# An attention and two-MLP kernel: planner latencies and keys exchanged, the low half of the probabilities written in one step

## The chip, the core and the metric

The kernel runs on one core of a Trainium2 chip. The metric is device time in microseconds. Engines are named PE (matmul), DVE (vector), ACT (scalar), POOL (GpSimd) and SP, whose queue issues all DMAs.

## The reference

Inputs `q`, `k`, `v` have shape (4, 8, 576, 64): 4 batches, 8 heads, 576 tokens. The weights are 512 x 2048 and 2048 x 512, twice, in float64.

```python
q_rot, k_rot = rotate(q), rotate(k)                 # rotary embedding
scores = (1 / sqrt(64)) * q_rot @ k_rot.T
attn = softmax(scores)                              # max subtracted, 1e-9 in the sum
x = (attn @ v) -> 2304 x 512
h = x @ w_in;  x = (h * sigmoid(1.702 * h)) @ w_out     # first MLP
h = x @ w_in2; y = where(h > 0, h, exp(min(h, 0)) - 1) @ w_out2   # second MLP
```

## The kernel before

**Numbers.** Every matmul operand is split into a high and a low float16 half; a product is the sum of three (high x high, high x low, low x high), so that float32 precision is nearly kept. Low halves are made on DVE as `value * scale - high`.

**Attention.** Work is cut into 144 *units*: a block of tokens `n` (two per batch, 320 or 256 tokens), a pair of heads `hp`, a chunk of 128 queries and one head of the pair (or the last 64 queries of both heads). A unit (`s_unit`) runs: scores on PE (L788) into one of 2 PSUM buffers, negative maximum on DVE (L792), bias on DVE (L796), exponential on ACT (L800) into one of 2 buffers E, two tiny steps on DVE (L807, L811), the normalised high half on ACT or DVE (L816, L820), the low half on DVE, and a DMA transpose from SP (L836, L839) into `et`. The tile `Ehl` holds 576 high columns and 576 low ones. The low part is stored turned: its last 64 keys come first (L830, 64 columns), then its first 512 (L829). After the transpose the nine 128-row slots of `et` are thus: high keys 0 to 511 in four slots, one slot with the 64 last high keys in its upper and the 64 last low keys in its lower half, and low keys 0 to 511 in four slots.

For each block and head pair, `av_unit` multiplies the nine slots by V in 28 matmuls (L982): high slots by both halves of V, low slots by V's high half. The tile `v16` holds V's two halves; its fifth slot has the last 64 keys twice, once per half of the partitions. V's high half is made on ACT (L764), its low half on DVE (L768), 16 times each (batch, head pair).

**Preparation.** `prep` runs 16 times: loads of q and k (L607, L608) into one buffer R, maximum (L614) and scale, rotation on DVE (L631, L635, L639), high halves on ACT (L653, L659), low halves on DVE (L664), and one transpose of 3840 columns into `qkT` (L681).

**MLPs.** Weights arrive as float64 bit patterns and are converted on ACT and DVE (L421 to L440), their maximum is taken, then they are split (L497 to L524). The raw weights of the first MLP pass through the tiles `gh` and `gl`, which the first MLP itself writes later: it can start only when the conversion of `w1o` is over. The first MLP runs block by block (L1028, then L1062), with L1031, L1035, L1039 and L1045 on ACT and DVE between. When attention is done its memory is given to the second MLP's weights (`open2`), which are then loaded, converted and split; the second MLP runs in blocks of 512 tokens (L1169, L1210).

**Order.** Each engine runs its instructions in program order, and that order is written by a planner (`Plan.run`): a list scheduler that gives each operation a price per engine and a key, and on an engine that is free starts the ready operation with the lowest key. An operation is ready when all its predecessors are over, which the planner puts a latency `lat` (345 ns; `lsame`, 218 ns, on the same engine) after their end. A DMA has its own latency plus `dlat`, 823 ns. The keys come from the table `TUNE`: for unit `i`, scores have `i - TUNE["s"]`, maxima `i - TUNE["mx"]`, high and low halves `i`. The first MLP's matmuls have 1e6 and more on PE, so they fill what attention leaves; their work on ACT and DVE has -1e5 to -9e4 and goes first.

Of the kernel before, what the change touches and what calls it, by code (L numbers as in the profile page):

```python
# [9 lines left out]
F16 = mybir.dt.float16  # L10
# [4 lines left out]
ALU = mybir.AluOpType  # L15
AX = mybir.AxisListType
P = 128
# [9 lines left out]
    pe_w1i=12, pe_w1o=0, lsame=218.42826132665004, tab=-30.0, f_dve=8.919624976581842, f_act=-17.90165985370676, f_pool=12.224437399728332,  # L27
    w2s=15.07761611796668, w1i2=30.204632970574707, w1o2=-73.74635818936522, dlat=823.3988909607715, qh=-8.32414955715731,
    kt=-6.667322173378593, vam=7.40425146733344, p0=2, lat=344.9241913205742, slack=1000000000.0, w1i=-56.15596474631266,
    w1i_s=2.8429601770045223, w1o=19.54548776828132, w1o_s=0.9651873495458939, prep0_s=1.3779993771618317, nt=5.6622832505119804,  # L30
    s_f=40.3256386921686, mx_f=6.7540349396707375, ex_f=7.075547533776429, av_f=14.806376760777082, prep0=29.665311617753602,
    prep=-52.798465949313695, va0=1.3429180038713335, va=-3.8436751296349594, vs=0.9879982807500122, tiny=0.9993537914172514,
    av=-30.965081688981684, ex=-2.7284093806181335, mx=2.7048753351162738, s=-9.997660299005439, tr=-10.34413763597054,
    bits=-9.409726003447773,
)
ORDER = ("pe", "act", "dve", "pool", "dma", "none")
# [6 lines left out]
class Plan:  # L43
# [12 lines left out]
    def op(self, eng, *args, port=False, **kw):  # L56


        lat = TUNE["lat"]
# [29 lines left out]
    def run(self):  # L89
# [10 lines left out]
        def start(e, now):  # L100
# [39 lines left out]
            busy[e] = end  # L140
            if e == "pool" or (e == "dve" and o.port):
                busy["port"] = end
            heapq.heappush(events, (end, o.seq, 0, e, None))
            if e != "dma":
                heapq.heappush(events, (end + min(TUNE["lsame"], o.lat), o.seq, 0.5, e, o))
            heapq.heappush(events, (end + o.lat, o.seq, 1, e, o))
# [76 lines left out]
def kernel(  # L223
# [63 lines left out]
    def buf(name, pool, shape, dt, n):  # L287
        plan.buffers(name, n)
        spec[name] = (pool, shape, dt)
# [27 lines left out]
    buf("v16", ap_, [P, 2, 5, 2, D], F16, BUFS["v16"])  # L317
    buf("x", per, [P, 2, NMAX], F16, BUFS["x"])
# [21 lines left out]
    def across(am, n, hM, after, key, add=False, use=()):  # L340
# [23 lines left out]
        o = op({"dve": 220.0 + 150.0 * (n > 1)}, most, [o], key, use=[hM], port=n > 1)  # L364
# [229 lines left out]
    def prep(b, hp):  # L594
# [109 lines left out]
        t = op(*dma_tr(3840), tr, [ql, kl], key - TUNE["kt"], need=[("qkT", hX)], use=[hN])  # L704
# [21 lines left out]
    def v_prep(b):  # L726
# [32 lines left out]
        for hp in range(NP):  # L759
            ks = last_u[fb[b], hp] - TUNE["vs"]  # L760
            h, hv = ("vs", b, hp), ("v16", b, hp)
# [551 lines left out]
```

## Time and profile before

| | us |
|---|---|
| median of 3 runs (1124.43 to 1135.83) | 1132.98 |
| the profiled execution | 1129.07 |
| its span, first to last instruction | 1127.3 |
| busy: PE / DVE / ACT / POOL | 976.1 / 826.4 / 638.4 / 12.3 |
| mean granted clock of PE, as a share of full speed | 0.954 |

A busy share over the whole span is a mean of stages with different limits, so the profile is read by stretches of time. A duration of an operation in the trace can overlap with that of the next on the same engine. A line number is that of the kernel before.

### The profile page before, as it was taken

To read this page: it belongs to the slowest core of one execution; us is meant where nothing else is said; L and a number is where in the kernel's file an instruction comes from. 1 tells how busy PE (TensorE), PEld (TensorE's weight loads), DVE (VectorE), ACT (ScalarE), POOL (GpSimd) and SP (SyncE) were. 2 spreads that over 40 slices of the span, in tenths; PEclk is the share of its full clock that TensorE was granted. 3 is DMA by queue.
4 is the path that set the end of the run, shared out by engine and by line. 5 is a ranking of instruction groups with operands and counts; after the bars stand their busy time and mean duration, and the time that the engine had idled before them with its cause. 6 is when DMAs were issued, how large, how long until landed. Compare 5 with 4: busy or idle time off the path is not lost.

```text
span 1127.3 us, 18484 instructions
## 1 busy us (share of the span) xinstructions
PE 976.1 (87%) x6710; PEld 615.7 (55%) x6710; DVE 826.4 (73%) x2070; ACT 638.4 (57%) x1237; POOL 12.3 (1%) x31
## 2 busy tenths in 40 slices
PE   1356669889858999989899999985999999999998
PEld 0123348656536667867588777732444444444474
DVE  7898899789978979989998679999227227237041
ACT  6588778566667757687475546785225125125041
POOL 2000000000000000000000000000000000000000
PEclk9988769999969989999999999998999999999999
DMA  9989743866756676664665553651000100000000
GB/s 303 227 202 246 148 92 72 161 129 130 171 136 108 148 154 137 126 147 102 139 125 115 144 167 101 191 164 38 19 19 1 47 19 1 28 19 1 19 20 19
DMA packets 287419, 122.19 MB, mean 108 GB/s; under 512 B 261728, under 2 KB 274656, under 8 KB 287328
## 3 DMA queue, kind: packets, MB, share of 16 engines
q1 hardware_dynamic: 287328, 121.02, 46.1%
q8 instruction: 52, 0.85, 0.3%
q14 instruction: 39, 0.32, 0.1%
HBM read 53.35 MB, written 9.44 MB: 56 GB/s over the span
## 4 chain that ended last, share of the span: by engine, by line
PE 43%; DVE 33%; DMA 13%; issue 4%; ACT 3%; SPq 3%; DVEq 0%; POOL 0%; POOLq 0%; ACTq 0%
PE m L1210 17%; PE m L1169 14%; PE m L1062 5%; DVE Ehl L829 4%; DMA qkT<-n 4%; DVE st L792 4%; DVE t L1035 3%; DVE gl L1045 3%; DMA R<-in_k_dram 3%; DMA et<-Ehl 3%; PE av L982 2%; PE m L1028 2%; PE s L788 2%; DVE n L664 2%; DMA R<-in_moe_w_in_dram 1%
## 5 line engine op out<-in xcount | busy, mean ns | idle before, releaser
L1062 PE MATMUL m<-gh,wo 128*128 128x256 f16 (+1 forms) x1024 | 203.0, 290 | 0.1
L1028 PE MATMUL m<-x,wi 128*128 128x256 f16 (+1 forms) x1536 | 198.2, 286 | 5.4 <-DVE t L1035 4.0
L1169 PE MATMUL m<-yhl,w2i 128*128 128x512 f16 (+1 forms) x960 | 188.5, 358 | 4.6 <-DVE e L1180 3.7
L1210 PE MATMUL m<-w2o,g 128*128 128x512 f16 x864 | 190.3, 382 | 0.0
L1028 PEld LDWEIGHTS <-wi 128*128 128x128 f16 x1536 | 149.0, 98 | 47.2 <-issue 9.9
L1062 PEld LDWEIGHTS <-wo 128*128 128x128 f16 x1536 | 150.7, 99 | 42.9 <-issue 3.6
L788 PE MATMUL s<-qkT 128*128 128x288 f16 (+1 forms) x640 | 104.4, 311 | 58.0 <-ACT E L800 41.1
L1062 PE MATMUL m<-gl,wo 128*128 128x256 f16 (+1 forms) x512 | 148.5, 290 | 0.0
L1169 PEld LDWEIGHTS <-w2i 128*128 128x128 f16 x960 | 93.8, 98 | 97.6 <-issue 5.7
L800 ACT ACTIVATE E<-s,st,qk_c 128x576 f32<-128x576 f32 x144 | 118.8, 826 | 43.2 <-DVE st L796 13.2
L1210 PEld LDWEIGHTS <-g 128*128 128x128 f16 x864 | 84.7, 99 | 102.8 <-issue 3.5
L1176 DVE TENSOR_SCALAR e<-e 128x512 f32<-128x512 f32 (+1 forms) x80 | 31.7, 397 | 147.1 <-ACT e L1172 147.1
L792 DVE TENSOR_REDUCE st<-s 128x1 f32<-128x576 f32 x144 | 107.2, 746 | 15.0 <-PE s L788 14.6
L829 DVE SCALAR_TENSOR_TENSOR Ehl<-E,st,Ehl 128x512 f16<-128x512 f32 x144 | 107.1, 744 | 10.5 <-ACT Ehl L816 10.1
L788 PEld LDWEIGHTS <-qkT 128*128 128x128 f16 (+1 forms) x640 | 57.4, 106 | 90.2 <-issue 55.5
L1213 ACT ACTIVATE o<-m,eo 128x512 f32<-128x512 f32 x18 | 12.4, 688 | 157.3 <-PE m L1210 157.3
L816 ACT ACTIVATE Ehl<-E,st 128x576 f16<-128x576 f32 x102 | 78.3, 770 | 38.0 <-issue 11.7
L1172 ACT ACTIVATE e<-m,y_c 128x512 f32<-128x512 f32 (+1 forms) x80 | 51.4, 643 | 52.1 <-PE m L1169 46.3
L982 PE MATMUL av<-et,v 128*64 128x320 f16 (+1 forms) x896 | 73.4, 316 | 3.8 <-DMA et<-Ehl 3.7
L1031 ACT ACTIVATE t<-m,hsc 128x256 f32<-128x256 f32 (+1 forms) x128 | 63.4, 496 | 23.3 <-PE m L1028 21.0
L1183 ACT ACTIVATE g<-e,y_c 128x512 f16<-128x512 f32 (+1 forms) x80 | 53.7, 675 | 25.0 <-DVE e L1180 24.5
L982 PEld LDWEIGHTS <-v 128*64 128x64 f16 x896 | 54.8, 121 | 19.4 <-issue 8.1
(164 smaller groups left out, 1136.7 us busy)
## 6 DMA issues: line engine op xcount, KB each, us to landing
R<-in_moe_w_in_dram SPq DMA_DIRECT2D x16, 512.0 KB, 4.7
R<-in_moe_w_out_dram SPq DMA_DIRECT2D x16, 512.0 KB, 4.3
gh<-in_moe_w_in_dram SPq DMA_DIRECT2D x8, 512.0 KB, 4.8
gl<-in_moe_w_in_dram SPq DMA_DIRECT2D x8, 512.0 KB, 5.8
R<-in_q_dram SPq DMA_DIRECT2D x16, 256.0 KB, 2.9
R<-in_k_dram SPq DMA_DIRECT2D x16, 256.0 KB, 3.5
V<-in_v_dram SPq DMA_DIRECT2D x32, 128.0 KB, 2.9
gh<-in_moe_w_out_dram SPq DMA_DIRECT2D x8, 512.0 KB, 4.2
```

The lines of the kernel that those rows point to most:

```text
L788: nc.tensor.matmul(o, X[:, a, t], X[:, 2 + 2 * x + a, cs], start=x == 0, stop=x == 1)
L792: nc.vector.tensor_reduce(out=st["t"][:, 0:1], in_=take(hS)[:, :, 0:NS], axis=AX.XY, op=ALU.max, negate=True)
L800: nc.scalar.activation(out=take(hE).rearrange("p (c f) -> p c f", c=2), in_=take(hS)[:, :, 0:NS], func=AF.Exp, bias=t[:, 1:2], scale=csc[b ...
L816: nc.scalar.activation(out=X16[:, 0:S], in_=take(hE), func=AF.Copy, scale=st["t"][:, 3:4])
L829: nc.vector.scalar_tensor_tensor(out=X16[:, S + TAIL:2 * S], in0=E[:, 0:512], scalar=r, in1=X16[:, 0:512], op0=ALU.mult, op1=ALU.subtract)
L982: nc.tensor.matmul(ps[64 * a:64 * a + 64, 0:N], V[:, w, j, a, :], T[:, a, blk, 0:N], start=i == 0, stop=i == len(slots) - 1)
L1028: nc.tensor.matmul(ps[:, 0:N], W1i.lhs(kk, u, wl), x[:, xl, 0:N], start=kk == 0 and i == 0, stop=kk == KD - 1 and i == 2)
L1031: nc.scalar.activation(out=take(ht)[:, 0:N], in_=take(hM)[:, 0:N], func=AF.Tanh, scale=hsc[b][:, 1:2])
L1062: nc.tensor.matmul(ps[:, 0:N], W1o.lhs(f, d, wl), (gh, gl)[xl][:, f, 0:N], start=f == 0 and i == 0, stop=f == KF - 1 and i == 2)
L1169: nc.tensor.matmul(ps[:, 0:n], W2i.lhs(kk, u, wl), Y[:, xl, kk, 0:n], start=kk == 0 and i == 0, stop=kk == KD - 1 and i == 2)
L1183: nc.scalar.activation(out=g2_tile()[:, u, 0:n], in_=take(he)[:, 0:n], func=AF.Copy, scale=st["c"][:, 1:2])
L1210: nc.tensor.matmul(ps, g[:, f, 512 * gi + P * tt:512 * gi + P * tt + P], W2o.h[:, f, 512 * wl:512 * wl + 512], start=f == 0 and i == 0, st ...
```

## The change

- The low half of the probabilities is written in key order, 576 columns in one DVE operation in place of 512 and 64. The fifth slot of `et` then holds the last 64 high keys and the *first* 64 low keys, and the four slots after it hold low keys 64 to 575.
- So V is needed shifted by 64 keys for the low slots. A new tile `vsh` (3 buffers) gets V's high half moved across the partitions by two DMAs from SBUF to SBUF, and a third DMA puts V's first 64 keys into the lower half of `v16`'s fifth slot. These three DMAs are issued on SP's queue after L768, 16 times; the attention output waits for them. The number of its matmuls stays 28.
- The planner's latency becomes one per engine (PE 230 ns, ACT 170, DVE 145, POOL 200), at most 125 on the same engine. The transpose into `qkT` is priced 4700 + 1800 ns in place of 3767 + 935, and a few other prices change.
- Most keys in `TUNE` change. `p0` = 1 cuts batch 0 into a block of 320 tokens and then one of 256, as the other batches; before it was 256, then 320.

```diff
--- before.py
+++ after.py
@@ -24,15 +24,16 @@
     s=2, av=1, m=3, E=2, Ehl=3, et=2, qkT=3, N16=1, R=1, V=4, T=1, v16=3, x=9, t=3, y=1, R2=3, yhl=1, mr=1, e=2, o=3,
 )
 TUNE = dict(
-    pe_w1i=12, pe_w1o=0, lsame=218.42826132665004, tab=-30.0, f_dve=8.919624976581842, f_act=-17.90165985370676, f_pool=12.224437399728332,
-    w2s=15.07761611796668, w1i2=30.204632970574707, w1o2=-73.74635818936522, dlat=823.3988909607715, qh=-8.32414955715731,
-    kt=-6.667322173378593, vam=7.40425146733344, p0=2, lat=344.9241913205742, slack=1000000000.0, w1i=-56.15596474631266,
-    w1i_s=2.8429601770045223, w1o=19.54548776828132, w1o_s=0.9651873495458939, prep0_s=1.3779993771618317, nt=5.6622832505119804,
-    s_f=40.3256386921686, mx_f=6.7540349396707375, ex_f=7.075547533776429, av_f=14.806376760777082, prep0=29.665311617753602,
-    prep=-52.798465949313695, va0=1.3429180038713335, va=-3.8436751296349594, vs=0.9879982807500122, tiny=0.9993537914172514,
-    av=-30.965081688981684, ex=-2.7284093806181335, mx=2.7048753351162738, s=-9.997660299005439, tr=-10.34413763597054,
-    bits=-9.409726003447773,
+    pe_w1i=12, pe_w1o=0, lsame=218.42826132665004, tab=-72.97, f_dve=158.19, f_act=8.42, f_pool=12.224437399728332,
+    w2s=195.33, w1i2=50.4, w1o2=-142.64, dlat=823.3988909607715, qh=-59.5,
+    kt=-32.02, vam=131.57, p0=1, lat=344.9241913205742, slack=1000000000.0, w1i=-51.38,
+    w1i_s=2.9, w1o=59.09, w1o_s=1.19, prep0_s=0.45, nt=5.6622832505119804,
+    s_f=40.3256386921686, mx_f=6.7540349396707375, ex_f=7.075547533776429, av_f=14.806376760777082, prep0=49.34,
+    prep=-60.31, va0=-39.21, va=-62.78, vs=0.59, tiny=2.79,
+    av=4.76, ex=-62.15, mx=-22.0, s=-24.23, tr=-61.89,
+    bits=-42.89,
 )
+LAT = {"pe": 230.0, "act": 170.0, "dve": 145.0, "pool": 200.0, "dma": 0.0, "none": 0.0}
 ORDER = ("pe", "act", "dve", "pool", "dma", "none")
 
 
@@ -56,7 +57,7 @@
     def op(self, eng, *args, port=False, **kw):
 
 
-        lat = TUNE["lat"]
+        lat = None
         if args and isinstance(args[0], float):
             lat, args = args[0] + TUNE["dlat"], args[1:]
         o = self.add(eng, *args, lat=lat, **kw)
@@ -138,12 +139,13 @@
             o.fn(e)
             end = now + o.eng[e]
             busy[e] = end
+            lat = LAT[e] if o.lat is None else o.lat
             if e == "pool" or (e == "dve" and o.port):
                 busy["port"] = end
             heapq.heappush(events, (end, o.seq, 0, e, None))
             if e != "dma":
-                heapq.heappush(events, (end + min(TUNE["lsame"], o.lat), o.seq, 0.5, e, o))
-            heapq.heappush(events, (end + o.lat, o.seq, 1, e, o))
+                heapq.heappush(events, (end + min(125.0, lat), o.seq, 0.5, e, o))
+            heapq.heappush(events, (end + lat, o.seq, 1, e, o))
             return True
 
         for o in self.ops:
@@ -315,6 +317,7 @@
     buf("mr", ap_, [6, 256], BF16, BUFS["mr"])
     buf("T", ap_, [P, 4, 5, D], F32, BUFS["T"])
     buf("v16", ap_, [P, 2, 5, 2, D], F16, BUFS["v16"])
+    buf("vsh", ap_, [P, 4, 2, D], F16, BUFS["v16"])
     buf("x", per, [P, 2, NMAX], F16, BUFS["x"])
     buf("t", per, [P, NMAX], F32, BUFS["t"])
     buf("y", per, [P, NMAX], F32, BUFS["y"])
@@ -361,7 +364,7 @@
             nc.tensor.matmul(take(hM)[:, 256:256 + n], square[0:n], st["d"][0:n] if n > 1 else st["r"][0:1], start=True, stop=True)
 
         o = op({"pe": 300.0}, turn, list(after) + [ready_c], key, need=[("m", hM)], use=use)
-        o = op({"dve": 220.0 + 150.0 * (n > 1)}, most, [o], key, use=[hM], port=n > 1)
+        o = op({"dve": 220.0 + 220.0 * (n > 1)}, most, [o], key, use=[hM], port=n > 1)
         return op({"pe": 200.0}, back, [o, lit], key, use=[hM])
 
     def max_scale(am, name, bufs, after, key, add=False, mul=1.0):
@@ -701,7 +704,7 @@
         else:
             kl = op({"dve": c_dve(640, k=2, ptr=2)}, k_lo, [kh], key, use=[hR, hN], port=True)
             ql = op({"dve": c_dve(640, k=2, ptr=2)}, q_lo, [qh], key, use=[hR, hN], port=True)
-        t = op(*dma_tr(3840), tr, [ql, kl], key - TUNE["kt"], need=[("qkT", hX)], use=[hN])
+        t = op({"dma": 4700.0}, 1800.0, tr, [ql, kl], key - TUNE["kt"], need=[("qkT", hX)], use=[hN])
         last_prep[:] = [ld]
         return [t, sc]
 
@@ -758,7 +761,7 @@
         v_scaled[b] = so
         for hp in range(NP):
             ks = last_u[fb[b], hp] - TUNE["vs"]
-            h, hv = ("vs", b, hp), ("v16", b, hp)
+            h, hv, hw = ("vs", b, hp), ("v16", b, hp), ("vsh", b, hp)
 
             def hi(e, hp=hp, hv=hv):
                 nc.scalar.activation(out=take(hv)[:, 0].rearrange("p j h d -> p (j h) d"), in_=v_view(b, hp)[:, :, 0:D], func=AF.Copy, scale=sc["s"])
@@ -767,7 +770,14 @@
                 X = take(hv).rearrange("p w j h d -> p w (j h) d")
                 nc.vector.scalar_tensor_tensor(out=X[:, 1], in0=v_view(b, hp)[:, :, 0:D], scalar=sc["s"], in1=X[:, 0], op0=ALU.mult, op1=ALU.subtract)
             o1 = op({"act": c_act(640, ptr=1)}, hi, [so], ks, need=[("v16", hv)], use=[h])
-            v_ready[b, hp] = op({"dve": c_dve(640, ptr=1) + 70}, lo, [o1], ks, use=[h, hv], port=True)
+
+            def shift(e, hv=hv, hw=hw):
+                X, Y = take(hv), take(hw)
+                nc.sync.dma_start(out=Y[0:64], in_=X[64:P, 0, 0:4])
+                nc.sync.dma_start(out=Y[64:P], in_=X[0:64, 0, 1:5])
+                nc.sync.dma_start(out=X[64:P, :, 4], in_=X[0:64, :, 0])
+            o2 = op({"dve": c_dve(640, ptr=1) + 70}, lo, [o1], ks, use=[h, hv], port=True)
+            v_ready[b, hp] = op(*dma_in(200e3, 3), shift, [o2], ks, need=[("vsh", hw)], use=[hv])
 
 
     x_ready = {}
@@ -823,11 +833,9 @@
             X16, E, r = take(hEl), take(hE), st["t"][:, 3:4]
             if e == "pool":
                 nc.gpsimd.tensor_scalar(out=E, in0=E, scalar1=r, scalar2=1.0, op0=ALU.mult, op1=ALU.mult)
-                nc.gpsimd.tensor_tensor(out=X16[:, S + TAIL:2 * S], in0=E[:, 0:512], in1=X16[:, 0:512], op=ALU.subtract)
-                nc.gpsimd.tensor_tensor(out=X16[:, S:S + TAIL], in0=E[:, 512:S], in1=X16[:, 512:S], op=ALU.subtract)
+                nc.gpsimd.tensor_tensor(out=X16[:, S:2 * S], in0=E, in1=X16[:, 0:S], op=ALU.subtract)
                 return
-            nc.vector.scalar_tensor_tensor(out=X16[:, S + TAIL:2 * S], in0=E[:, 0:512], scalar=r, in1=X16[:, 0:512], op0=ALU.mult, op1=ALU.subtract)
-            nc.vector.scalar_tensor_tensor(out=X16[:, S:S + TAIL], in0=E[:, 512:S], scalar=r, in1=X16[:, 512:S], op0=ALU.mult, op1=ALU.subtract)
+            nc.vector.scalar_tensor_tensor(out=X16[:, S:2 * S], in0=E, scalar=r, in1=X16[:, 0:S], op0=ALU.mult, op1=ALU.subtract)
 
         def tr(e):
             X16, T = take(hEl), take(hT)
@@ -860,7 +868,7 @@
         if FLEX["Elo"]:
             o7 = op({"dve": c_dve(S, k=2, ptr=2), "pool": 2250}, lo, [o6], key, use=[hE, hEl], port=True)
         else:
-            o7 = op({"dve": c_dve(S, k=2, ptr=2)}, lo, [o6], key, use=[hE, hEl], port=True)
+            o7 = op({"dve": c_dve(S, ptr=1)}, lo, [o6], key, use=[hE, hEl], port=True)
         fst = i == first_u[n, hp]
         cost = dma_tr(2 * S) if h is not None else ({"dma": 2350}, 1300.0)
         trs.append(op(*cost, tr, [o7] + trs[:1], key - TUNE["tr"], need=[("et", hT)] if fst else (), use=[hEl] + ([] if fst else [hT])))
@@ -972,14 +980,14 @@
 
     def av_unit(n, hp, trs, st):
         b, chunks, tail, n0, N = blocks[n]
-        hT, hV, hA, hx = ("et", n, hp), ("v16", b, hp), ("av", n, hp), ("x", n, hp)
-        slots = [(j, w, j) for j in range(4) for w in range(2)] + [(4, 0, 4), (4, 1, 4)] + [(5 + j, 0, j) for j in range(4)]
+        hT, hV, hW, hA, hx = ("et", n, hp), ("v16", b, hp), ("vsh", b, hp), ("av", n, hp), ("x", n, hp)
+        slots = [(j, w, j) for j in range(5) for w in range(2)] + [(5 + j, 2, j) for j in range(4)]
 
         def mm(e):
-            T, V, ps = take(hT), take(hV), take(hA)
+            T, V, W, ps = take(hT), take(hV), take(hW), take(hA)
             for i, (blk, w, j) in enumerate(slots):
                 for a in range(2):
-                    nc.tensor.matmul(ps[64 * a:64 * a + 64, 0:N], V[:, w, j, a, :], T[:, a, blk, 0:N], start=i == 0, stop=i == len(slots) - 1)
+                    nc.tensor.matmul(ps[64 * a:64 * a + 64, 0:N], W[:, j, a, :] if w == 2 else V[:, w, j, a, :], T[:, a, blk, 0:N], start=i == 0, stop=i == len(slots) - 1)
 
         def hi(e):
             nc.scalar.activation(out=take(hx)[:, 0, 0:N], in_=take(hA)[:, 0:N], func=AF.Copy, scale=DOWN)
@@ -989,7 +997,7 @@
             nc.vector.scalar_tensor_tensor(out=x[:, 1, 0:N], in0=take(hA)[:, 0:N], scalar=DOWN, in1=x[:, 0, 0:N], op0=ALU.mult, op1=ALU.subtract)
 
         key = float(last_u[n, hp]) - TUNE["av"]
-        o = op({"pe": 14 * (N / 2.0 + 6)}, mm, trs + [v_ready[b, hp]], key, need=[("av", hA)], use=[hT, hV])
+        o = op({"pe": 14 * (N / 2.4 + 4)}, mm, trs + [v_ready[b, hp]], key, need=[("av", hA)], use=[hT, hV, hW])
         o = op({"act": c_act(N, True)}, hi, [o], -1e4, need=[("x", hx)], use=[hA])
         x_ready[n, hp] = op({"dve": c_dve(N)}, lo, [o], -1e4, use=[hA, hx])
```

## Rows read from the trace of the kernel before

**Rows 1.** The page: its first line and busy time by engine.
```profile
span 1127.3 us, 18484 instructions
PE 976.1 (87%) x6710; PEld 615.7 (55%) x6710; DVE 826.4 (73%) x2070; ACT 638.4 (57%) x1237; POOL 12.3 (1%) x31
```

**Rows 2.** Stretches: us, busy us of PE, PEld, DVE, ACT, POOL (count), clock, DMA share, GB/s.
```profile
0.00:163.00 163.00, 78.56 (x472) 42.57 (x473) 143.43 (x359) 117.27 (x214) 8.90 (x20) 0.84 0.84 210
163.00:627.00 464.00, 421.60 (x3614) 317.44 (x3612) 410.38 (x1182) 313.44 (x656) 3.38 (x11) 0.96 0.64 130
627.00:728.00 101.00, 98.13 (x800) 76.63 (x799) 87.31 (x172) 61.54 (x126) 0.00 (x0) 1.00 0.48 147
728.00:787.00 59.00, 41.44 (x190) 17.99 (x188) 57.20 (x114) 42.35 (x77) 0.00 (x0) 0.93 0.38 118
787.00:1127.00 340.00, 336.36 (x1642) 161.08 (x1642) 128.05 (x247) 103.79 (x165) 0.00 (x0) 0.99 0.06 18
...
163.00:350.00 187.00, 157.44 (x1307) 115.58 (x1305) 163.93 (x466) 123.85 (x255) 1.53 (x5) 0.93 0.63 128
350.00:627.00 277.00, 264.16 (x2309) 201.86 (x2308) 246.46 (x717) 189.59 (x402) 1.84 (x6) 0.98 0.64 131
```

**Rows 3.** Single lines: duration ns min/median/max, first and last start in us.
```profile
L1028 PE MATMUL m<-x,wi x1536: 269/290/474, 161.8 to 702.8; 128*128 128x256 f16 x96, 128*128 128x320 f16 x96
...
L989 DVE SCALAR_TENSOR_TENSOR x<-av,x x32: 403/452/490, 94.0 to 630.0; 128x256 f16<-128x256 f32 x16, 128x320 f16<-128x320 f32 x16
...
L440 DVE SCALAR_TENSOR_TENSOR wo<-wo,gl x8: 674/684/703, 81.5 to 126.4; 128x512 int32<-128x512 int32 x8
...
L1210 PE MATMUL m<-w2o,g x864: 379/379/634, 787.5 to 1123.0; 128*128 128x512 f16 x173
```

**Rows 4.** Timeline of DVE from 240 us: start us, duration us, operation.
```profile
240.28 0.74 DVE L829 SCALAR_TENSOR_TENSOR Ehl<-E,st,Ehl 128x512 f16<-128x512 f32 x1
240.94 0.28 DVE L830 SCALAR_TENSOR_TENSOR Ehl<-E,st,Ehl 128x64 f16<-128x64 f32 x1
241.14 0.75 DVE L792 TENSOR_REDUCE st<-s 128x1 f32<-128x576 f32 x1
```

**Rows 5.** Waits of DVE, 163 to 627: total us, times, longest us.
```profile
DVE T L631 <- DMA R<-in_k_dram: 11.0, 8, 2.5
DVE st L792 <- PE s L788: 10.6, 16, 3.5
```

**Rows 6.** Waits of PE, 163 to 627.
```profile
PE s L788 <- DMA qkT<-n: 12.8, 7, 2.9
```

**Rows 7.** DMA issues: KB each, median us from issue to landing.
```profile
et<-Ehl SPq DMA_TRANSPOSE x160, 2.9
V<-in_v_dram SPq DMA_DIRECT2D x32, 32.0 KB, 2.5
qkT<-n SPq DMA_TRANSPOSE x16, 7.3
```

**Rows 8.** Timeline from 252 us, DVE and ACT.
```profile
252.38 1.48 DVE L639 TENSOR_TENSOR R<-R,T 128x1280 f32<-128x1280 f32 x1
...
253.90 1.36 ACT L653 ACTIVATE n<-R,qk_s 128x1280 f16<-128x1280 f32 x1 [1.06 <-DVE R L639]
```

**Rows 9.** The issues of one line on SP's queue.
```profile
L739 SPq DMA_DIRECT2D V<-in_v_dram x32: 612/622/892, 12.1 to 414.0; - x32
```

**Rows 10.** Stretches of L829 on DVE alone: us, busy us (count), clock, DMA share, GB/s.
```profile
0.00:163.00 163.00, 18.62 (x25) 0.84 0.84 210
163.00:200.00 37.00, 6.39 (x9) 1.00 0.36 75
```

## The prediction

> **What bounds the kernel now.** The profiled execution took 1129.07 us, of which 1127.3 are the span [rows 1]; 1.8 us lie around it. It stands 3.9 us under the median of the runs, 1132.98. I cost against 1129.07 and state the result on that footing.
>
> The whole-span shares (PE 87%, DVE 73%) [rows 1] hide three stages, so I cut the span at the events that separate them: the first L1028 matmul at 161.8, the last attention output (L989) at 630.0, and the first L1210 matmul at 787.5 [rows 3]. Busy time by stretch [rows 2] then reads as follows.
> - 0 to 163: DVE 143.4 of 163, PE 78.6. Weight conversion, preparation and the first 25 or 26 of the 144 units of attention; PE has little to do because L1028 may not start.
> - 163 to 627: DVE 410.4 of 464 (88%), PE 421.6 (91%). Neither is full. DVE is the tighter at first (163.9 of 187 against PE's 157.4 up to 350), PE later (264.2 of 277 against 246.5).
> - 627 to 787: DVE 144.5 of 160 (87.3 + 57.2), PE 139.6 (98.1 + 41.4). PE works off two blocks of the first MLP and the first matmuls of the second, while DVE converts the second MLP's weights and ends last.
> - From 787: PE 336.4 of 340. Nothing of the change is in there, and its order keys stay.
>
> So the end is reached 340 us after the moment at which L1210 may start, and that comes 160 us after attention's end. PE has 160 - 139.6 = 20.4 us of idle in those 160. An earlier end of attention therefore passes to the end for about 20 us even if PE recovers none of its idle time before; beyond that, PE's 42.4 idle us between 163 and 627 must shrink too.
>
> **The change, part by part.**
>
> **Low half in one step.** Per unit, L829 (512 columns) and L830 (64) become one operation of 576. Their recorded durations, 0.74 and 0.28, overlap with the next operation's; what counts is the distance between starts on the busy engine: 240.28, 240.94, 241.14 [rows 4], that is 0.66 + 0.20 = 0.86 us for the pair. Both steps fit one line: 448 more columns cost 0.46 us, so 64 columns cost 0.066 and the fixed part is about 0.134. One step of 576 is then 0.66 + 0.066 = 0.73; 0.13 us saved. 144 x 0.13 = 18.7 us of DVE, 3.4 of them before 163. By durations it would be 0.28 - 0.066 = 0.21 and 30.3 us: the upper bound. I take the spacing, since it is what the next instruction sees. The Trainium skill (VectorE: DVE Perf Modes, section on the TRN2 errata) gives SBUF-to-SBUF work a fixed 58 cycles at 0.96 GHz, which by estimate would leave 144 x 0.06 = 8.7 us. By that rule the sum below would be 10 us worse; the trace's 0.134 disagrees with it, as does the page's own remark of some 150 cycles measured.
>
> If DVE keeps its 88% share, 18.7 us of work shorten its stretch by up to 21; I count 18.7, inside the 20.4 that pass through the stage after attention. High halves, exponentials, transposes and the 28 matmuls per block of attention output keep their number and shape: no change on ACT and PE.
>
> **Shifted values.** 16 times, three SBUF copies follow the low half of V. They put 48 issues on SP's queue at about 0.62 us each (the V loads at L739) [rows 9]: 16 x 1.9 = 30 us of SP, spread over attention. In this queue each group waits for L768 on DVE; behind it stand transposes of Ehl and loads of q, k, V, and for those wait Ehl's next writer (ACT L816), the attention output (PE) and the rotation on DVE. Landing: no row shows an SBUF-to-SBUF copy. The nearest is a 32 KB V load, 2.5 us after its issue [rows 7], so about 2.5 + 1.3 = 3.8 us after the first issue until the third has landed. The planner books 1.44 + 1.35 + 0.82 = 3.61 us (its price, its latency and `dlat`), close to that. The cover is the last unit's own transposes, 2.9 us each [rows 7], which the same matmuls await anyway, and MLP matmuls on PE. I take 0. If nothing covers them, 16 x 3.8 = 61 us of waits at most, of which PE's other work absorbs most; a gain is excluded, since they add work only.
>
> **Latencies.** The planner charged 0.345 us from any engine to another. In the trace L639 starts at 252.38; the planner books 1.40 us for it, and the waiting L653 starts at 253.90 [rows 8]: 0.12 us after the booked end, against 0.145 in the new table. The old plan was therefore late by 0.2 us per hand-over. That cost engines little: an instruction planned late sits behind other work, and DVE was 88% busy. The qkT transpose errs the other way. It was booked as 3.77 + 1.76 = 5.5 us and lands in 7.3 [rows 7]; the new 4.70 + 2.62 = 7.3 matches. PE's scores wait for it 12.8 us between 163 and 627 [rows 6] and DVE's maxima wait 10.6 us for scores [rows 5]. These are the waits that the better plan can remove. Gain between 0 and 12.8 + 10.6 = 23.4; I take half of the first, 6.4, because a removed wait on one in-order queue mostly exposes the next one, here q/k landing before L631 (11.0 us) [rows 5].
>
> **New keys.** These only reorder. For DVE the maxima drop from i - 2.7 to i + 22 while low halves stay at i, so open units are finished before new ones start; PE's attention output moves from last_u + 31 to last_u - 4.8, ahead of scores (i + 24). With two score and two E buffers, few units are open, so I cost this at 0, with -10 to +10 for it, about the size of one class of wait in rows 5. Preparation of batch 0 moves ahead of most of W1i, W1o's loads move back (from 19.5..34 to 59..77), and batch 0's first block is 320 wide instead of 256, so its x comes after 20 units instead of 16. In the trace of before x was not what L1028 waited for: W1o's conversion ended at 126.4 and its scaling had to follow [rows 3]. I cost it at 0; its bad case is the third rival.
>
> **Sum:** 1129.1 - 18.7 - 6.4 = 1104.0.
>
> **The rivals.**
> 1. *PE becomes full.* DVE's saving, the qkT waits and PE's idle time all go. From 163 PE has 421.6 + 98.1 + 41.4 + 336.4 = 897.6 us of work in 964; 66.7 us are idle. If two thirds of that vanish: 1129 - 45 = 1084. For it: PE is starved up to 350 (29.6 of 187 idle) because blocks of attention arrive slowly, and that is where DVE is tightest. Against it: the waits named in rows 5 and 6 are many small ones.
> 2. *The saving is taken back on the way.* DVE's 18.7 us turn into idle time before T (L631), whose loads stand on SP behind the new waits, or before the attention output. SP's extra 30 us against DVE's 18.7 show that it can happen. Time: 1129 less half of the qkT correction (3), about 1126.
> 3. *First MLP starts late: slower.* W1o's conversion now ranks behind all 36 units of batch 0 (keys up to 57). Before, about 35 units had been done at 200 us (25 by 163, 9 in the next 37) [rows 10]. If conversion waited that long, L1028 would start 161.8 - 126.4 = 35 us later, at about 235. PE's remaining work, 897.6 less some 10 of attention already done, then ends at 1122 without any idle time and at 1156 with half of the 66.7 idle us. It costs over 1% (11 us) from a start at 163 + (33 + 11)/0.86 = 214, where 0.86 takes off the 10 in 72 us of attention done meanwhile. For it: the order of the keys. Against it: DVE has 19.6 idle us before 163, into which conversions fall because the planner starts any ready work, and faster attention repays part of a late start.
>
> That the change does not do what it says I rule out for the low half (one instruction less is plain in the code); for the latencies rows 8 agree.
>
> **How the numbers follow.** About 1% is what a measurement here can tell from no change. Forecast 0.52 (own range 1085 to 1118), rival 1 0.14, rival 2 0.19, rival 3 0.15. Faster by over 1%: 0.52 + 0.14 = 0.66; within 1%: 0.19; slower: 0.15. Lowest sum: 1129 - 30.3 - 23.4 = 1075, with 3 more for the order. The range takes 1072 to 1140: below it rival 1's best, above it most of rival 3, together 2 in 10.
>
> **What will show it.** The 576-wide step at about 0.73 us from start to start and DVE's sum lower by some 19 us; L989's last start near 605 to 612; L1028's first start between 155 and 185; the gap from there to L1210's first start still about 160; the qkT wait of PE's scores below 6 us; shifted copies landing within 4 us with no attention output waiting over 1 us for them. I am wrong if attention's end moves and L1210's start does not, if L1028 starts past 214, or if SP's queue becomes what T and the attention output wait for.

## The result and the profile after

The kernel after took 1077.68 us (median of 4 runs, 1076.59 to 1078.97) against 1129.97 us for the kernel before, run beside it (4 runs, 1124.43 to 1135.83): ratio 0.9537, 95% interval 0.9482 to 0.9593. The change saves 52 us where 25 were forecast. Direction and range held. The time lies near the lower end of the range, which was made that wide for the first rival, so the hit says little for the sum; the size was off by more than a factor of two. Theories and intervals below are judged against the kernel before as it ran on the same chip each time (medians from 1129.69 to 1132.16 us). Two changed kernels often ran on different chips, so a difference between them can be off by some 2 us, the spread of these medians.

The profiled execution after took 1078.97 us. The first line of its page and its busy times, to be held against [rows 1]:

```profile
span 1077.2 us, 18378 instructions
...
PE 964.2 (90%) x6710; PEld 612.2 (57%) x6710; DVE 791.0 (73%) x1886; ACT 655.0 (61%) x1277; POOL 8.2 (1%) x31
```

The kernel's lines have moved by 8 or so: L1036 was L1028, L997 was L989, L1218 was L1210, L798 was L788 (scores), L838 is the new low half, L826 and L830 are the high half on ACT and on DVE (they were L816 and L820). First the three events that cut the stages, as in [rows 3]:

```profile
L1036 PE MATMUL m<-x,wi x1536: 269/291/310, 175.9 to 670.4; 128*128 128x320 f16 x96, 128*128 128x256 f16 x96
...
L997 DVE SCALAR_TENSOR_TENSOR x<-av,x x32: 405/452/493, 88.0 to 583.8; 128x320 f16<-128x320 f32 x16, 128x256 f16<-128x256 f32 x16
...
L1218 PE MATMUL m<-w2o,g x864: 376/379/390, 736.8 to 1073.0; 128*128 128x512 f16 x173
```

Attention's end came forward by 46.2 us (630.0 to 583.8) and the second MLP's start by 50.7 (787.5 to 736.8); the span fell by 50.1. So the saving is made before attention ends and passes through to the end. Busy time by stretch, cut at these events (columns as in [rows 2]):

```profile
0.00:176.00 176.00, 87.52 (x526) 48.42 (x526) 151.43 (x371) 136.59 (x253) 5.18 (x21) 0.84 0.91 215
176.00:581.00 405.00, 387.95 (x3417) 295.08 (x3415) 368.94 (x989) 309.42 (x649) 3.06 (x10) 1.00 0.73 145
581.00:691.00 110.00, 110.00 (x925) 88.74 (x923) 92.81 (x179) 70.35 (x146) 0.00 (x0) 1.00 0.51 158
691.00:737.00 46.00, 43.83 (x207) 19.84 (x205) 44.49 (x91) 34.27 (x61) 0.00 (x0) 1.00 0.28 82
737.00:1077.00 340.00, 334.95 (x1644) 160.10 (x1642) 133.31 (x259) 104.42 (x170) 0.00 (x0) 1.00 0.08 21
```

Subtract PE's busy time from each stretch. Idle PE during attention falls from 42.4 us [rows 2] to 17.05, and between attention and the second MLP from 20.4 to 2.2; ahead of the first MLP it grows from 84.4 to 88.5, in the last stretch from 3.6 to 5.05. Together that is 38.2 us less. The other 11.9 of the 50.1 are PE's own busy time (976.1 to 964.2, at the same 6710 matmuls): its granted clock was 0.96 during attention before and is 1.00 now. PE is full from the first MLP matmul to the end: 24.3 us idle in 901, against 66.5 in 964.

The two waits that the prediction singled out [rows 5, 6], in the waits of PE and then of DVE, 176 to 581 us (total us, times, longest us):

```profile
PE av L990 <- DMA et<-Ehl: 6.8, 8, 1.7
PE s L798 <- ACT E L810: 5.4, 12, 1.0
PE s L798 <- DMA qkT<-n: 2.3, 2, 1.2
```

```profile
DVE T L634 <- DMA R<-in_k_dram: 5.2, 7, 1.2
...
DVE st L802 <- PE s L798: 1.0, 1, 1.0
```

Scores wait 2.3 us for the qkT transpose instead of 12.8, and DVE's maxima wait 1.0 us for scores instead of 10.6. DVE's wait for k's landing, which the prediction expected to be exposed in their place, fell from 11.0 to 5.2. PE's longest wait of that stretch in the kernel before is not in the prediction: scores waited for the exponential, which has to read the score buffer first, 163 to 627 us:

```profile
PE s L788 <- ACT E L800: 16.2, 14, 4.1
```

It fell to 5.4. DVE's busy time fell by 35.4 us, not 19. Two groups show where most of it went, by form (count, busy us, mean ns, then idle before with its releasers). Before:

```profile
L816 ACT ACTIVATE Ehl<-E,st 128x576 f16<-128x576 f32 x102 | 78.3, 770 | 38.0 <-issue 11.7 <-DMA et<-Ehl 9.1 <-DVE st L796 8.6
...
L820 DVE TENSOR_SCALAR Ehl<-E,st 128x576 f16<-128x576 f32 x42 | 21.5, 513 | 0.9 <-DMA et<-Ehl 0.4
```

After:

```profile
L838 DVE SCALAR_TENSOR_TENSOR Ehl<-E,st,Ehl 128x576 f16<-128x576 f32 x144 | 116.1, 810 | 10.6 <-ACT Ehl L826 10.1
L826 ACT ACTIVATE Ehl<-E,st 128x576 f16<-128x576 f32 x127 | 97.2, 770 | 36.1 <-DMA et<-Ehl 19.6 <-DVE st L821 4.9 <-issue 2.9
L830 DVE TENSOR_SCALAR Ehl<-E,st 128x576 f16<-128x576 f32 x17 | 8.8, 517 | 3.5 <-DMA et<-Ehl 3.2
```

25 of the high halves, which either engine may do, moved from DVE to ACT (42 to 17): 12.7 us of DVE that the prediction never costed. Weight conversions, splits and maxima that moved the same way make some 7 more. Two of the new keys, `f_dve` (8.9 to 158.2) and `f_act` (-17.9 to 8.4), are the offsets by which the planner chooses the engine; putting them back is one of the experiments. Also to be kept from these rows: ACT's high half now waits 19.6 us for `et<-Ehl`, the transpose that has to read the buffer first; it was 9.1.

The shifted copies land soon after issue (DMA issues: count, KB each, median us from issue to landing; [rows 7]):

```profile
vsh<-v SPq DMA_DIRECT2D x32, 64.0 KB, 2.0
v<-v SPq DMA_DIRECT2D x16, 32.0 KB, 1.9
...
qkT<-n SPq DMA_TRANSPOSE x16, 7.0
```

### The profile page after: what moved, and what is told of

It reads as the page before. It is cut to its first block, busy times and chain, and to the rows that moved or that the text cites. A ratio compares the mean times of both kernels' runs of the same rounds, so it can differ in the third digit from the quotient of the medians.

```text
span 1077.2 us, 18378 instructions
## 1 busy us (share of the span) xinstructions
PE 964.2 (90%) x6710; PEld 612.2 (57%) x6710; DVE 791.0 (73%) x1886; ACT 655.0 (61%) x1277; POOL 8.2 (1%) x31
## 4 chain that ended last, share of the span: by engine, by line
PE 52%; DVE 25%; DMA 11%; ACT 5%; issue 3%; SPq 3%; POOL 0%; DVEq 0%; ACTq 0%; POOLq 0%
PE m L1218 16%; PE m L1177 14%; PE m L1070 9%; DMA et<-Ehl 6%; PE m L1036 6%; PE av L990 4%; DVE Ehl L838 3%; DMA R<-in_k_dram 3%; PE s L798 3%; DVE st L802 3%; DVE t L1043 2%; DVE gl L1053 2%; DVE n L667 2%; ACT E L810 1%; DVE T L634 1%
## 5 line engine op out<-in xcount | busy, mean ns | idle before, releaser
L1036 PE MATMUL m<-x,wi 128*128 128x320 f16 (+1 forms) x1536 | 198.1, 286 | 1.8 <-ACT y L1076 0.9
L1070 PE MATMUL m<-gh,wo 128*128 128x256 f16 (+1 forms) x1024 | 198.5, 286 | 0.0
L1218 PE MATMUL m<-w2o,g 128*128 128x512 f16 x864 | 189.1, 379 | 1.4 <-ACT w2o L500 0.8
L1036 PEld LDWEIGHTS <-wi 128*128 128x128 f16 x1536 | 148.7, 98 | 42.4 <-issue 5.4
L1070 PEld LDWEIGHTS <-wo 128*128 128x128 f16 x1536 | 148.5, 98 | 40.2 <-issue 3.5
L1070 PE MATMUL m<-gl,wo 128*128 128x320 f16 (+1 forms) x512 | 146.3, 286 | 0.0
L1218 PEld LDWEIGHTS <-g 128*128 128x128 f16 x864 | 84.1, 98 | 102.5 <-issue 2.7
L810 ACT ACTIVATE E<-s,st,qk_c 128x576 f32<-128x576 f32 x144 | 118.7, 825 | 23.4 <-DVE st L806 17.4
L798 PE MATMUL s<-qkT 128*128 128x288 f16 (+1 forms) x640 | 102.2, 310 | 27.1 <-ACT E L810 24.5
L838 DVE SCALAR_TENSOR_TENSOR Ehl<-E,st,Ehl 128x576 f16<-128x576 f32 x144 | 116.1, 810 | 10.6 <-ACT Ehl L826 10.1
L826 ACT ACTIVATE Ehl<-E,st 128x576 f16<-128x576 f32 x127 | 97.2, 770 | 36.1 <-DMA et<-Ehl 19.6
L798 PEld LDWEIGHTS <-qkT 128*128 128x128 f16 (+1 forms) x640 | 58.0, 105 | 65.3 <-issue 48.0
L1195 DVE SCALAR_TENSOR_TENSOR g<-e,y_c,g 128x512 f16<-128x512 f32 (+1 forms) x80 | 55.5, 694 | 28.3 <-ACT g L1191 27.5
L1039 ACT ACTIVATE t<-m,hsc 128x320 f32<-128x320 f32 (+1 forms) x128 | 63.4, 496 | 10.2 <-PE m L1036 9.7
L1047 ACT ACTIVATE gh<-t 128x320 f16<-128x320 f32 (+1 forms) x128 | 55.5, 439 | 10.0 <-DVE t L1043 9.7
```

The lines of the kernel that those rows point to most:

```text
L798: nc.tensor.matmul(o, X[:, a, t], X[:, 2 + 2 * x + a, cs], start=x == 0, stop=x == 1)
L810: nc.scalar.activation(out=take(hE).rearrange("p (c f) -> p c f", c=2), in_=take(hS)[:, :, 0:NS], func=AF.Exp, bias=t[:, 1:2], scale=csc[b ...
L826: nc.scalar.activation(out=X16[:, 0:S], in_=take(hE), func=AF.Copy, scale=st["t"][:, 3:4])
L838: nc.vector.scalar_tensor_tensor(out=X16[:, S:2 * S], in0=E, scalar=r, in1=X16[:, 0:S], op0=ALU.mult, op1=ALU.subtract)
L1036: nc.tensor.matmul(ps[:, 0:N], W1i.lhs(kk, u, wl), x[:, xl, 0:N], start=kk == 0 and i == 0, stop=kk == KD - 1 and i == 2)
L1039: nc.scalar.activation(out=take(ht)[:, 0:N], in_=take(hM)[:, 0:N], func=AF.Tanh, scale=hsc[b][:, 1:2])
```

## The experiments

**Theory A**, the prediction's: the 576-wide low half gives the larger part, planning the smaller. **Theory B**: the plan gives nearly all. Four kernels split the change.

*Low half and copies alone, old keys and latencies.* Edit: all of the diff's lines in the low half, the shift and the attention output; `TUNE`, latencies and the other prices as before.

> The low half in one step with the shifted values, on the kernel before; keys, latencies and all other prices as before. Theory A (DVE work sets attention's end; the 18.7 us of the step come out at the end): 1107 to 1114 us against 1130. Theory B (the gain came from the planner's latencies and keys, DVE work is covered): within 6 us of 1130. DVE's sum should be 17 to 20 us lower than before under both.

Measured 1137.91, ratio 1.0062 [1.0039, 1.0085]: slightly slower than the kernel before, 5.8 us beside its 1132.16. A falls for this order. DVE's busy time fell by 11.9 us (826.4 to 814.5), less than expected under both theories: in this plan 16 operations fewer ran on ACT (1237 to 1221).

*Plan alone.* Edit: the kernel after with the low half in two steps and without shifted values.

> The changed kernel with the two-step low half put back: new keys, latencies and prices alone. Theory A: 1077 + 19 to 25, that is 1096 to 1102 us. Theory B: 1077 to 1085 us.

Measured 1087.98, ratio 0.9613 [0.958, 0.9645]: 44 us under the kernel before beside it, between the two ranges. B stands for most of the gain; the 10 us to the kernel after are its rest.

*Old offsets in the new kernel.*
```
-f_dve=158.19, f_act=8.42
+f_dve=8.919624976581842, f_act=-17.90165985370676
```

> The changed kernel with the two offsets for operations that may run on several engines put back (f_dve 8.9, f_act -17.9), all else new. Theory A: some 25 high halves and 6 weight splits return to DVE, about 16 us of work, 1077 + 12 to 18 = 1089 to 1095 us. Theory B: 1077 to 1083 us.

*New offsets in the old kernel*: the same edit in the other direction.

> The kernel before with only these two offsets new (f_dve 158.2, f_act 8.4). Theory A: DVE loses some 16 us of work to ACT, 1112 to 1120 us. Theory B: within 6 us of 1130.

Measured 1102.47 (0.974 [0.9711, 0.9768]) and 1111.56 (0.9812 [0.9776, 0.9848]). The first lies above both ranges, the second at the edge of A's. The offsets are worth 25 us when undone and some 20 when done alone. In the second kernel 10 high halves (102 to 112 on ACT) and some weight work changed engine, and DVE's busy time fell by 9.8 us (826.4 to 816.6). The saving is twice that, so it is not DVE's load alone. The order round these operations changes too, and no run takes the two apart.

That made the next question whether any change of order moves this kernel, and what the low half is worth with the order held.

*A nudge of the order.* Edit to the kernel before: `lat=344.9` to `lat=340.0`.

> The kernel before with the planner's latency 340 ns in place of 344.9: nothing is better or worse in it, but the order of thousands of instructions is another. Theory A and L and K alike if order is harmless in itself: within 3 us of 1132. If any new order costs or brings time by chance: off by 4 to 15 us, either way; e1_low_only's loss would then be of that kind.

Measured 1129.8, 0.9987 [0.9963, 1.0011]. One other order with no better prices is worth nothing. It is a single sample: the low half with copies took 1137.91 above and takes 1144.37 below in another order, 6 us apart. That the differences of 15 us and more below are not the scatter of reordering is likely by this, and not shown.

*Low half and copies, every engine's order as before.* The planner keeps the old price, and the copies are issued inside the operation of V's low half:
```
-o7 = op({"dve": c_dve(S, ptr=1)}, lo, ...
+o7 = op({"dve": c_dve(S, k=2, ptr=2)}, lo, ...
-v_ready[b, hp] = op(*dma_in(200e3, 3), shift, [o2], ks, ...
+def lo_shift(e, lo=lo, shift=shift):
+    lo(e)
+    shift(e)
```

> The low half in one step and the shifted values on the kernel before, with every engine's order of before kept: the planner still books the old price, and the three copies are issued right after V's low half without being planned. Theory A (DVE's time counts; in e1_low_only the new order took it back): 1110 to 1121 us against 1132. Theory B (the saved time is covered by other waits whatever the order): 1128 to 1138 us.

*The same without copies.* Edit: `shift(e)` left out, unshifted V in the four last slots.

> As e5_low_same_order (order of before kept), but the three copies are not issued and the low slots are multiplied by the unshifted values, so the low part of the attention output is left wrong. Theory S (the copies on SP's queue eat what the step saves): 1113 to 1124 us. Theory C (in the old order the saved DVE time is covered, other waits end last): 1128 to 1134 us.

*The same with copies and two steps* (512 and 64 columns, in key order).

> As e5_low_same_order, but the low half is written in two steps of 512 and 64 columns as before, in key order: the copies alone, in the order of before. Theory S: e5's 1144 plus the step's 15 to 19, that is 1158 to 1164 us. Theory C: 1142 to 1150 us.

Measured 1144.37 (1.0111 [1.0068, 1.0153]), 1126.26 (0.9957 [0.9932, 0.9983]) and 1146.24 (1.0126 [1.009, 1.0161]). The first lies above both its ranges, the second between S and C, the third in C's. In the old order the one step is worth 4 us without copies (1130.5 to 1126.3) and 2 with them (1146.2 to 1144.4, no more than the intervals allow for nothing). The copies cost 16 with two steps (1130.5 to 1146.2, on one chip) and 18 with one (1126.3 to 1144.4). Where DVE's time went is in the kernel without copies, 163 to 627 us, its stretch and then its waits:

```profile
163.00:627.00 464.00, 424.59 (x3657) 320.13 (x3655) 399.45 (x1067) 313.91 (x660) 3.37 (x11) 0.96 0.65 130
```

```profile
DVE st L803 <- PE s L799: 17.0, 23, 3.1
DVE T L634 <- DMA R<-in_k_dram: 12.1, 7, 3.3
```

DVE is busy 399.45 us instead of 410.38, and its two old waits grew from 10.6 and 11.0 [rows 5] to 17.0 and 12.1. A shorter instruction reached the same late scores and loads sooner and waited: rival 2 of the prediction, here for the low half alone. What the copies do is in ACT's waits, 0 to 640 us, without them and with them:

```profile
ACT Ehl L827 <- DMA et<-Ehl: 10.4, 8, 2.7
```

```profile
ACT Ehl L828 <- DMA et<-Ehl: 17.2, 9, 5.1
```

*Copies and low half in the new order.* Three kernels with the order after: low half in two steps; the copies not issued (unshifted V); the copies on POOL's queue, with all of the computation done:
```
-nc.sync.dma_start(out=Y[0:64], in_=X[64:P, 0, 0:4])
+nc.gpsimd.dma_start(out=Y[0:64], in_=X[64:P, 0, 0:4])
... (and the two others)
```

> The changed kernel with its order kept and the low half written in two steps of 512 and 64 columns: 19 us more of DVE work in the new order. If DVE's time counts in full in the new order: 1093 to 1098 us. If it is covered there too: 1078 to 1084 us.

> The changed kernel with its order kept, the three copies not issued and the low slots multiplied by the unshifted values (the low part of the attention output is left wrong). Theory S: the copies cost something here too, 1065 to 1073 us. If the new order covers them: 1075 to 1079 us.

> The changed kernel with its order kept and the three copies issued from POOL's queue instead of SP's. If the copies cost because they stand on SP's queue in front of the transposes (which then free Ehl late, so that ACT's high half waits): 1066 to 1072 us, ACT's wait for the transposes down from 19.6 us to 9 to 12. If they cost because the attention output waits for their landing, or because of the DMA engines: 1075 to 1085 us.

Measured 1088.08 (0.9614 [0.9582, 0.9646]), 1068.02 (0.9438 [0.9411, 0.9465]) and 1073.65 (0.9502 [0.947, 0.9534]). Against the 1077.68 of the kernel after, the one step is worth 10.4 us in the new order, the copies still cost 9.7, and moving them off SP's queue gives 4.0 of those back. The second alone fell into one of its ranges (S); the two others lie between theirs. The interval of the kernel without copies lies wholly below that of the kernel after; those of the two others touch it, so 10.4 and 4.0 are less sure. The copies land in 2.0 us on SP's queue, and no wait of the attention output for them is listed. Its wait for `et<-Ehl`, the transposes, is. ACT's wait for these transposes and then PE's, 0 to 600 us, with the copies on SP's queue, on POOL's, and not issued:

```profile
ACT Ehl L826 <- DMA et<-Ehl: 19.6, 14, 3.4
```

```profile
ACT Ehl L826 <- DMA et<-Ehl: 13.9, 8, 3.4
```

```profile
ACT Ehl L823 <- DMA et<-Ehl: 9.5, 7, 3.0
```

```profile
PE av L990 <- DMA et<-Ehl: 8.8, 12, 1.7
```

```profile
PE av L990 <- DMA et<-Ehl: 3.9, 8, 1.1
```

```profile
PE av L987 <- DMA et<-Ehl: 2.9, 4, 1.3
```

Both waits fall in the order of the times. Copies stand ahead of transposes of Ehl: Ehl is freed later, ACT's next high half is held, and the attention output gets its transposed slots later. With the copies on POOL's queue ACT's wait does not fall all the way, and 4.0 of the 9.7 us come back. Why the rest stays is open: that the copies still hold something through POOL's order, through their later landing there (3.1 us) or through the DMA engines wasn't separated. That kernel, 1073.65, is the fastest of those that compute everything.

With the order held, the copies take what the step brings, or more: 2 to 4 us against 16 to 18 in the old order, 10.4 against 9.7 in the new. So the 10 us from the plan alone (1087.98) to the kernel after must lie mostly in the order that the planner writes when the low half is booked shorter. No run shows that order by itself.

*Which of the prices and keys.* Before with the new latencies and all new prices; after with the old ones; before with these and the offsets:

> The kernel before with the new latencies and prices alone; keys and low half of before. Theory L (truer latencies make the better order): 1095 to 1118 us. Theory K (the keys make it, of them the offsets some 20 us): 1125 to 1140 us.

> The changed kernel with the old latencies and prices in the planner (345 ns, 218 on the same engine, the transpose into qkT at 5.5 us); keys and low half new. Theory L: 1093 to 1110 us. Theory K: 1074 to 1086 us.

> The kernel before with the new latencies, prices and the two engine offsets; all other keys and the low half of before. If the two parts that brought 20 us each simply add up: 1090 to 1096 us, and the other keys bring what is left to e2's 1088, at most 8. If they overlap: 1100 to 1112 us, and the other keys are worth 12 to 24.

Measured 1111.85 (0.9823 [0.9799, 0.9848]), 1116.34 (0.9869 [0.984, 0.9898]) and 1109.02 (0.9815 [0.9778, 0.9852]). The first and the third are in the ranges of L and of overlap, the second is above both of its ranges. Latencies and prices are worth 20 us alone (1131.74 beside it) and 39 when undone. With the offsets on top, 3 more, by the ratios 1: the parts overlap. That leaves 21 (1109.0 to 1088.0) for the other keys.

*The qkT price by itself.* In the kernel before, and taken back in the kernel after:
```
-t = op(*dma_tr(3840), tr, ...
+t = op({"dma": 4700.0}, 1800.0, tr, ...
```

> The kernel before with only the transpose into qkT booked at 7.3 us instead of 5.5. My term for it was 6.4 us: 1122 to 1128 us, and PE's waits for this transpose down from 12.8 us to under 5. If the removed waits only expose the next ones: 1129 to 1133 us.

> The changed kernel with only the transpose into qkT booked at 5.5 us again. If that price brings in the new plan what it brought alone (24 us): 1098 to 1106 us. If the new keys start the scores late enough anyway: 1077 to 1086 us.

Measured 1105.46 (0.9781 [0.9751, 0.9811]), that is 24 us from one booked duration, and 1111.61 (0.9841 [0.9826, 0.9856]), 34 us lost when it is undone. Both lie outside both of their ranges, on the side where the price counts for more. Of the first kernel, PE's and DVE's waits around scores, 0 to 640 us, then its events and PE's busy time:

```profile
PE s L788 <- ACT E L800: 28.2, 25, 3.7
...
PE av L982 <- DMA et<-Ehl: 6.4, 8, 2.0
...
PE s L788 <- DMA qkT<-n: 1.8, 2, 1.0
```

```profile
DVE st L792 <- PE s L788: 5.1, 11, 1.3
```

```profile
L989 DVE SCALAR_TENSOR_TENSOR x<-av,x x32: 415/448/492, 90.3 to 612.6; 128x256 f16<-128x256 f32 x16, 128x320 f16<-128x320 f32 x16
...
L1210 PE MATMUL m<-w2o,g x864: 379/379/634, 761.8 to 1097.0; 128*128 128x512 f16 x173
```

```profile
span 1101.3 us, 18492 instructions
...
PE 963.0 (87%) x6710; PEld 611.9 (56%) x6710; DVE 824.3 (75%) x2066; ACT 637.9 (58%) x1236; POOL 12.8 (1%) x31
```

In the kernel before, over the same 640 us, these waits are:

```profile
PE s L788 <- ACT E L800: 41.1, 25, 4.1
...
PE s L788 <- DMA qkT<-n: 16.6, 9, 2.9
...
PE av L982 <- DMA et<-Ehl: 3.7, 8, 1.0
```

```profile
DVE st L792 <- PE s L788: 14.6, 19, 3.5
```

The two that the prediction named shrink by 14.8 and 9.5, 24.3 together. The agreement with the 24 us is luck. The two lie on different engines, scores wait 12.9 us less for the exponential too, and the attention output waits 2.7 us more. And the waits are only half of it: against the kernel before the span fell by 26.0 us (1127.3 to 1101.3), of which 13.1 are PE's busy time (976.1 to 963.0, the same 6710 matmuls) and 12.9 its idle time. Attention ends 17.4 us earlier (612.6), the second MLP starts 25.7 earlier (761.8). In the kernel after with the old price the waits are back, 0 to 600 us (24.5 and 2.3 in the kernel after):

```profile
PE s L798 <- ACT E L810: 31.2, 22, 3.7
...
PE s L798 <- DMA qkT<-n: 7.8, 7, 2.2
```

*The last two parts, undone in the new kernel*: `p0=2` instead of 1, and the old latencies with the new prices.

> The changed kernel with batch 0 cut as before (256 tokens first, then 320). If the first block's width does not matter, since the weights set the first MLP's start: 1074 to 1082 us. If the later first block of the changed kernel cost something: 1062 to 1073 us; if the new keys need it: above 1083 us.

> The changed kernel with the old latencies between engines (345 ns, 218 on the same engine) and all new prices. If e7's 39 us were mostly the transpose's price: 1080 to 1092 us. If the new keys hang on the new latencies: 1100 to 1116 us.

Measured 1097.24 (0.9716 [0.9678, 0.9753]) and 1093.11 (0.9685 [0.9661, 0.9709]): 20 and 15 us lost. The first is in the range "if the new keys need it", the second between its two ranges. What the two parts bring without the other keys these runs do not show. With the old keys the latencies and the other prices bring nothing: all new prices and latencies gave 1111.85, the qkT price alone 1105.46.

One way through the parts adds up by construction: 1130 to 1105.5 (qkT price), 1111.9 (latencies and the other prices), 1109.0 (offsets), 1088.0 (the other keys), 1077.7 (low half with copies, and the order that goes with them). Another order of taking them gives other shares; undone one at a time they come to 34, 25, 20, 15 and 10, twice the whole.

## Why the prediction was wrong in size

**The stage and the pass-through: right.** The forecast said that an earlier end of attention passes for about 20 us through PE's idle time after it, and beyond that only if PE's idle time during attention shrinks as well. The first gave 18.2 us (20.4 to 2.2), the second 25.4 (42.4 to 17.05). The gap from attention's end to the second MLP was 153 us, against 160 forecast.

**Low half: mis-sized by half.** The distance between starts came out as read off the old trace:

```profile
307.65 0.81 DVE L838 SCALAR_TENSOR_TENSOR Ehl<-E,st,Ehl 128x576 f16<-128x576 f32 x1
308.38 0.14 DVE L817 TENSOR_SCALAR st<-st 128x1 f32<-128x1 f32 x1
```

That is 0.73 us. With the order held, DVE's busy time differs by 16.8 us in the old order (828.7 to 811.9, both with copies) and by 15.5 in the new (806.5 to 791.0), a little under the 18.7 of the sum. The step that failed is the next one, "if DVE keeps its 88% share". In the old order it did not: 2 to 4 us reached the end. In the new one 10 did. On the size of the step itself: the Trainium skill (VectorE: DVE Perf Modes, section on the TRN2 errata) has a fixed 58 cycles, by which 576 columns would by estimate start 0.66 us apart; the 0.73 measured disagrees, and agrees with the fixed 0.134 us read off the old trace.

**Shifted values at 0: wrong.** The landing was rightly bounded (2.0 us against 3.8), and the prediction named the 30 us of issues on SP's queue and that ACT's high half waits behind them. It then priced only the landing. The copies cost 16 to 18 us in the old order and 10 in the new, of which some 4 go with SP's queue. The issue itself takes no more than the 0.62 us assumed, 0.53 in the median for the first of three (ns min/median/max, first and last start):

```profile
L776 SPq DMA_DIRECT2D vsh<-v x16: 515/534/1451, 74.9 to 540.3; - x16
```

**qkT price at 6.4: the term that was mis-sized most.** Both waits were found, and the upper bound of 23.4 written down. Half of one of them was taken, "because a removed wait on one in-order queue mostly exposes the next one". This is the step of the sum that failed. It measured 24.3 alone, and the reason given does not hold. The next wait in line, for k's landing, was not exposed but fell as well (11.0 to 5.2 in the kernel after, 6.5 with the price alone). Both waits have one cause: scores that the plan put too early stood at the head of PE's queue, and the MLP's matmuls and DVE's maxima stood behind them. Moving them later fills the hole with work that was ready: PE is busy 439.2 of the 464 us instead of 421.6. The bound of 23.4 was none, since it left out PE's longest wait in the stretch, 16.2 us for the exponential, which shrank as well (41.1 to 28.2 over 640 us). And PE's own busy time, which the sum holds fixed, fell by 13.1. A nearer estimate from the same rows was at hand, though by its path it too would have been right by luck: 16 transposes, each 1.8 us late (7.3 less 5.5), make 28.8.

**Latencies at 0: right with the old keys, as far as the runs show, wrong with the new**, where the old latencies lose 15 us.

**New keys at 0, -10 to +10: wrong.** `f_dve` and `f_act` stand in the diff and are not in the prediction; they alone move the old kernel by 20. On top of prices and offsets the other keys gave 21, `p0` some part of that. Which of these keys do it, and by which wait, stays open. "These only reorder" held as a rule for a nudge (1129.8) and not for the keys of this change.

**The rivals.** Rival 1, PE becomes full, is what happened: it had "two thirds" of 66.7 idle us vanish and 1084; 42.2 of 66.5 vanished (63%). That its 1084 lies near is in part luck, since PE's busy time fell by 11.9 too, which it did not foresee. It got 0.14, because the waits "are many small ones". They were many, but one price alone took away 17.6 of PE's 42.4 idle us from 163 to 627 us (to 24.8). Rival 2 is right of the low half alone and wrong of the whole. Rival 3's late start came about mildly, 175.9 instead of 161.8, far from 214, and cost nothing visible, since idle PE ahead of it grew by 4.0 only.

**The signs.** Spacing 0.73, first L1036 at 175.9 (155 to 185), gap 153, qkT wait 2.3 (below 6) and copies within 4 us came as written. Attention's end at 583.8 (605 to 612) and DVE's 35.4 (19) did not, and these two point at what was left out: the operations moved to ACT and the idle time.

## What to carry to other kernels

Where a planner writes the order of in-order queues, read its booked duration against the trace for every kind of operation that something waits on: an underbooked transpose cost 24 us here, where the shorter instruction brought 4 in the same order. Cost all waits behind one cause as one term, and go through the diff's keys one by one, above all those that move work between engines. A transfer that lands in time is still to be costed by what stands behind it in its queue, and another queue is to be tried (4 of 10 us here).

## What the runs showed of the hardware

The one surprise was how starved stretches cost PE twice. In the kernel before, PE was busy 5.45 of the 10 us from 310 and 3.83 of the 10 from 320, and the granted clock of these stretches was 0.61 and 0.73, means of its two levels, 1.2 and 2.4 GHz (0.5 and 1.0 of full speed):

```profile
310.00:320.00 10.00, 5.45 (x42) 3.65 (x43) 6.57 (x22) 4.99 (x10) 0.00 (x0) 0.61 0.32 80
320.00:330.00 10.00, 3.83 (x17) 1.84 (x16) 9.74 (x29) 7.33 (x13) 0.31 (x1) 0.73 0.62 141
```

Scores of one shape, PE's timeline from 320 us:

```profile
320.31 0.65 PE L788 MATMUL s<-qkT 128*128 128x288 f16 x4 [1.35 <-ACT E L800]
321.50 0.65 PE L788 MATMUL s<-qkT 128*128 128x288 f16 x4 [0.54 <-ACT E L800]
326.23 1.12 PE L788 MATMUL s<-qkT 128*128 128x288 f16 x4 [4.08 <-ACT E L800]
```

After an idle stretch of 4.08 us the same four matmuls took 1.12 instead of 0.65. With the qkT price alone changed, PE is busy 7.62 and 9.02 us in the same two stretches, and the clock stays at 1.00 there and over 163 to 627 us (columns as in [rows 2]):

```profile
310.00:320.00 10.00, 7.62 (x80) 5.62 (x75) 9.96 (x29) 7.38 (x16) 0.31 (x1) 1.00 0.64 142
320.00:330.00 10.00, 9.02 (x66) 6.07 (x64) 8.07 (x25) 8.04 (x20) 0.00 (x0) 1.00 1.00 177
163.00:627.00 464.00, 439.23 (x3833) 334.07 (x3831) 423.80 (x1211) 324.15 (x683) 3.37 (x11) 1.00 0.67 136
```

So a removed wait returned matmul time as well: at the same 6710 matmuls PE's busy time fell by 13.1 of the 26.0 us of span here, and by 11.9 of 50.1 in the kernel after. How much of that is the clock no run separates, since none changes the clock alone.
